# Layer 2's spatial product as seven block products over pairs of row tiles, with its mixer's pools on the other side of the memory

## The chip, the cores and the metric

The kernel runs on one core of a Trainium2 chip. A core has TensorE (PE, with its weight loads PEld), VectorE (DVE), ScalarE (ACT), GpSimd (POOL) and SyncE (SP), which here issues every DMA from one queue in order, and 16 DMA engines. The metric is the device time of one execution in microseconds (us), as the median of repeated runs.

## What is computed

Two layers, each a memory-augmented attention followed by a gated mixer (gMLP), on x of 2048 rows by 640. The change concerns the second layer's mixer:

```
z  = gelu(layernorm(x) @ w_in)        # 2048 x 1728
z1 = z[..., :864]
z2 = layernorm(z[..., 864:])
g  = einsum("ts,bsf->btf", w_sp, z2) + b_sp[None, :, None]     # w_sp 2048 x 2048
x  = x + einsum("bsf,fd->bsd", z1 * g, w_out)                  # w_out 864 x 640
```

Every matrix is split into a high and a low f16 part, and a product is three matmul passes: high by high, high by low, low by high.

## The kernel before

A layer runs in three phases. `phase1a` is the attention. `phase1b` (L234) projects the last four row tiles' attention (`yp`), normalizes each of the 16 row tiles of 128 rows, transposes it by DMA (`th`, L218) and multiplies it with w_in in two halves (`w_in_half`, L294): `z2_half` applies gelu and the layer norm and keeps z2 in SBUF as `zh` and `zl`, `z1_half` stores z1 to memory. TensorE's order is the written one, with the scheduler's moves by priority; the other engines' order is the scheduler's.

`phase2` (L326) goes over the 16 row tiles of w_sp. `rows` loads 128 rows (`wr`, 1 MB, L354), takes each row's largest value (L356) and a power-of-two scale from it (L346 to L361), splits the scaled rows into `wn` in two halves of 1024 columns (ACT L366, DVE L367) and transposes both by DMA into `wt` (L368). `spatial` multiplies: 16 blocks of 128 rows of z2, three passes, two halves of 432 columns, 96 matmuls into `gp` (L379). ACT adds the bias and scale (L382), DVE multiplies with z1 (L384), takes the row's largest value (L386), and ACT and DVE split the result into `un` (L392, L393), which a DMA transposes into `ut` (L395). `tail` multiplies `ut` with w_out (42 matmuls, L408), one tile behind, adds x1 (L411) and stores the output (L412). The next tile's `rows` are issued behind this tile's `spatial`. w_out's parts (`wuh`, `wul`, L106) load at the phase's start.

The pools of `attn_weights` and `kept_tiles` (the attention's weights and state) stay open to the program's end, and layer 2's phases take the memory above them.

## Time and profile before

| | |
|---|---|
| median of 3 runs | 2429.87 us (2422.15 to 2431.55) |
| the profiled execution, its own time | 2432.53 us |
| its span | 2430.8 us, granted clock 0.972 |
| layer 2: last score product of the attention | 1821.28 us |
| layer 2: first matmul with w_in | 1828.69 us |
| layer 2: first matmul of the spatial product | 2035.56 us |
| layer 2: last matmul | 2426.30 us |

The times of the last four rows are starts on TensorE's timeline, from the span's start. In the rows that follow, a name such as `wt<-wn` is the tile written and the tile read; L379 is line 379 of the kernel before. A bracket in a timeline's row gives the idle time of that engine just before it and what ended it. In rows of grouped instructions the count comes first, then busy us, the mean duration in ns, and the idle time before.

### The profile page before, as it was taken

How to read it: one execution, taken by the hardware profiler on the slowest of the kernel's cores; microseconds unless marked ns; L12 is line 12 of the kernel's file. 1: busy time of each engine (PE TensorE's matmuls, PEld its weight loads, DVE VectorE, ACT ScalarE, POOL GpSimd, SP SyncE). 2: the span in 40 equal slices, each digit the busy share in tenths (PEclk: the TensorE clock that was granted, in tenths of full speed). 3: DMA queues.
4: the chain of work that ended last, by engine and by line, in shares of the span. 5: the costliest groups of instructions: out<-in, count | busy, mean ns of one | idle time of the engine just before them, and what ended most of it. 6: DMA issues, size and time to landing. Idle time of an engine off the chain costs nothing. (4 is left out here: it accounts for less than half of the span.)

```text
span 2430.8 us, 50694 instructions
## 1 busy us (share of the span) xinstructions
PE 2222.3 (91%) x20682; PEld 1322.2 (54%) x20682; DVE 1437.1 (59%) x2765; ACT 1133.3 (47%) x1388; POOL 934.0 (38%) x723
## 2 busy tenths in 40 slices
PE   5778899999899999999997989999979997999998
PEld 2445555666555445555654556566654554555554
DVE  7678878776654545444226787887764453444431
ACT  3378688777632322211124987877762221211110
POOL 2178688888610100000002988898871010000000
PEclk9989899999999999999999999999999999999999
DMA  5653545455644388766334354454445345775662
GB/s 158 165 137 98 131 115 132 130 132 135 177 112 128 108 224 200 176 148 163 87 85 106 84 142 121 114 116 110 138 141 127 91 111 153 167 176 152 173 130 54
DMA packets 502505, 325.00 MB, mean 134 GB/s; under 512 B 408512, under 2 KB 443456, under 8 KB 497152
## 3 DMA queue, kind: packets, MB, share of 16 engines
q1 hardware_dynamic: 502272, 321.76, 51.8%
q8 instruction: 162, 2.65, 0.5%
q14 instruction: 71, 0.58, 0.1%
HBM read 148.25 MB, written 85.34 MB: 96 GB/s over the span
## 5 line engine op out<-in xcount | busy, mean ns | idle before, releaser
L975 POOL TENSOR_TENSOR PL<-P,PH 128x1280 f16<-128x1280 f32 x248 | 649.5, 2621 | 112.6 <-ACT PH L974 102.3
L379 PE MATMUL gp<-zh,wt 128*128 128x432 f16 x2048 | 465.3, 347 | 24.3 <-DMA wt<-wn 24.3
L964 DVE TENSOR_REDUCE mx<-mp 128x2 f32<-128x1024 f32 (+3 forms) x512 | 409.2, 817 | 109.7 <-PE mp L920 107.9
L379 PEld LDWEIGHTS <-wt 128*128 128x128 f16 x3072 | 301.1, 98 | 285.5 <-DMA wt<-wn 26.4
L957 ACT ACTIVATE P<-es,sc 128x1024 f32<-128x1024 f32 (+1 forms) x384 | 370.7, 965 | 136.1 <-PE es L920 134.0
L974 ACT CAST PH<-P 128x1280 f16<-128x1280 f32 x256 | 320.6, 1254 | 21.9 <-PE pv L1001 14.7
L294 PEld LDWEIGHTS <-th 128*128 128x128 f16 x1920 | 188.7, 98 | 177.6 <-issue 11.4
L394 POOL MEMSET un<- 128x64 f16 x32 | 4.9, 152 | 706.3 <-DMA ut<-un 645.9
L379 PE MATMUL gp<-zl,wt 128*128 128x432 f16 x1024 | 271.8, 347 | 0.0
L204 POOL TENSOR_TENSOR lnrs<-lnve,mhalf 128x1 f32<-128x1 f32 x92 | 56.5, 622 | 472.7 <-DVE lnve L203 447.6
L948 PEld LDWEIGHTS <-qk 60*128 60x128 f16 (+1 forms) x2048 | 91.3, 94 | 225.0 <-issue 156.2
L356 DVE TENSOR_REDUCE am<-wr 128x1 f32<-128x2048 f32 x32 | 73.2, 2286 | 228.3 <-DMA wr<-in_B_w_sp_dram 228.3
L382 ACT ACTIVATE u<-gp,bsp,un 128x864 f32<-128x864 f32 x32 | 34.2, 1070 | 365.6 <-PE gp L379 365.6
L408 PE MATMUL cyp<-wuh,ut 128*128 128x320 f16 (+1 forms) x896 | 168.4, 305 | 17.4 <-DMA ut<-un 17.4
L948 PE MATMUL mp<-qk 60*128 60x512 f16 (+3 forms) x1024 | 138.8, 308 | 40.7 <-DVE mx L964 39.7
L408 PEld LDWEIGHTS <-ut 128*128 128x128 f16 (+1 forms) x1344 | 133.5, 100 | 77.3 <-DMA ut<-un 19.8
L1001 PE MATMUL pv<-vs,PL 128*128 128x41 f16 x2560 | 164.6, 182 | 8.2 <-DVE PL L975 4.3
L1001 PE MATMUL pv<-vs,PH 128*128 128x41 f16 x2560 | 168.5, 183 | 3.3 <-DVE ab L1017 3.2
L725 PE MATMUL vps<-wvh,xt 128*128 128x320 f16 x640 | 157.5, 313 | 13.1 <-DMA xt<-xnhl 11.9
L920 PEld LDWEIGHTS <-big 64*128 64x128 f16 x3072 | 141.4, 95 | 51.4 <-issue 5.1
L948 PE MATMUL es<-qk 64*128 64x512 f16 (+3 forms) x1024 | 135.3, 300 | 35.3 <-ACT P L957 25.7
L366 ACT ACTIVATE wn<-wr,ivw 128x1024 f16<-128x1024 f32 x64 | 72.0, 1146 | 184.7 <-DVE ivw L361 111.1
(203 smaller groups left out, 4153.6 us busy)
## 6 DMA issues: line engine op xcount, KB each, us to landing
wr<-in_B_w_sp_dram SPq DMA_DIRECT2D x32, 1024.0 KB
...
```

What stands on the lines that cost most here:

```text
L294: nc.tensor.matmul(zp[:, n, :FHH], a[:, k, :], b[:, k, c:c + FHH], start=(k == 0 and j == 0), stop=(k == KD - 1 and j == 2))
L356: nc.vector.tensor_reduce(am, wr, AX.X, ALU.max, apply_absolute_value=True)
L379: nc.tensor.matmul(gp[:, n, :FHH], wt[:, k // 8, a, k % 8, :], b[:, k, n * FHH:(n + 1) * FHH], start=(k == 0 and j == 0), stop=(k == NT - ...
L408: nc.tensor.matmul(yp[:, n, :320], a[:kn[k], k, :], b[:kn[k], k, n * 320:(n + 1) * 320], start=(k == 0 and j == 0), stop=(k == KO - 1 and ...
L725: nc.tensor.matmul(ps, a[:, k, c], b[:, k, n * 320:(n + 1) * 320], start=(i == 0), stop=(i == 14))
L920: nc.tensor.matmul(out, g.big[r, 64 - 64 * s:192 - 64 * s], mk, start=False, stop=s == 1, skip_group_check=True)
L948: nc.tensor.matmul(out[:, h, o:o + w], a[r, ac], b[r, bc], start=o == 0, stop=False, skip_group_check=True)
L957: self.last_of["ACT"] = nc.scalar.activation(P[:, :, 512 * c:512 * c + ew], es[:, :, :ew], AF.Exp, scale=g.esc).ins
L964: self.last_of["DVE"] = nc.vector.tensor_reduce(self.mx[m][:, :, i], mp[:, :, o:o + w], AX.X, ALU.max).ins
L974: nc.scalar.copy(PH, P[:, h])
L975: (nc.gpsimd if h == 0 or n < self.N - self.TAIL else nc.vector).tensor_tensor(PL, P[:, h], PH, ALU.subtract)
L1001: nc.tensor.matmul(pv[:, i, h, :], x[:, c:c + 128], v[:, j, h0 + h, :], start=(j == 0 and x is PH), stop=(j == i and x is PL), skip_group_ ...
```

## The change

Rows and columns of w_sp are paired by tiles: of a pair of row tiles, `a11` and `a12` are the first tile's blocks of even and odd column tiles, `a21` and `a22` the second's. z2 is blocked the same way: even and odd row tiles, and its left and right 432 columns. The 2x2 block product, of eight block products, is done with seven (`product`, 24 matmuls of 432 columns each) on sums and differences of the blocks. The results are joined in PSUM, where some products accumulate on others, and by ACT and DVE (`scaled`, `plus`). For w_sp the four additions of a pair are GpSimd's (`mix`), on rows that ACT has scaled in place, and each of seven blocks is split and transposed by itself (`turned`): seven DMA transposes of a pair, where there were four. For z2 they are made in phase 1b as each tile is finished (`blocks`): seven arrays `zb` in the place of `zh` and `zl`, with four GpSimd differences a pair. Blocks are made seven products ahead of their use; there are eight `wt` buffers, two of `wn`, two of `wr`, one of `un`. SP's order in the new phase is the written one.

Layer 2's attention weights and state are closed when its attention ends (`ats.close()`); phase 1b's pools lie on the other side of the memory, and one tile `w0` over the closed pools holds first half of w_in and later w_out. The first layer is as before.

```diff
+    def place(self, t):
+        n = self.nk * self.cols
+        self.h, self.l = [t[:, i, :n].rearrange("p (k c) -> p k c", k=self.nk) for i in range(2)]
...
-def phase1b(g, o_d, x, x1_d, z1_d, zh, zl):
+def phase1b(g, o_d, x, x1_d, z1_d, put, w0=None):
     nc, tc = g.nc, g.tc
+    zs = ZS if w0 is None else ZB
     with ExitStack() as ctx:
         pool = lambda n, b, **k: ctx.enter_context(tc.tile_pool(name=n, bufs=b, reuse_waits="tile", **k))
-        p2, p1, px2, px1, sp = pool("b2", 2), pool("b1", 1), pool("bx2", 2), pool("bx1", 3 if g.wi[0].made else 1), pool("bs", 2)
-
-        pe2, pe1, wp0 = pool("be2", 2), pool("be1", 1), pool("bw0", 1)
+        if w0 is None:
+            p2, p1, px2, px1, sp = pool("b2", 2), pool("b1", 1), pool("bx2", 2), pool("bx1", 1), pool("bs", 2)
+            pe2, pe1, wp0 = pool("be2", 2), pool("be1", 1), pool("bw0", 1)
+        else:
+            right = lambda n, b: pool(n, b, side="right")
+            pe2, pe1, p2, p1, px2, px1, sp = right("be2", 2), right("be1", 1), right("b2", 2), right("b1", 2), right("bx2", 2), right("bx1", 3), None
...
         ctx.enter_context(tc.manual_schedule(engines=ENGINES))
-        g.wi[0].tiles(wp0)
-        with tc.high_priority(offset=HP):
+        if w0 is None:
+            g.wi[0].tiles(wp0)
+        else:
+            g.wi[0].place(w0)
+        with tc.high_priority(offset=HP if w0 is None else 2 * HP):
...
             z2 = p1.tile([128, FH], F32, tag="z2", name="z2")
-            nc.scalar.activation(z2.rearrange("p (n c) -> p n c", n=2), zp[:, :, :FHH], AF.Gelu_apprx_tanh, scale=g.zi[1])
-            layernorm(g, z2, z2, FH, 2, ZS)
-            nc.scalar.copy(zh[:, t, :], z2)
-            nc.vector.tensor_tensor(zl[:, t, :], z2, zh[:, t, :], ALU.subtract)
+            i = nc.scalar.activation(z2.rearrange("p (n c) -> p n c", n=2), zp[:, :, :FHH], AF.Gelu_apprx_tanh, scale=g.zi[1])
+            j = layernorm(g, z2, z2, FH, 2, zs)
+            put(t, z2, p1)
+            return i.ins, j.ins
...
-            z2_half(t, w_in_half(1, *th))
+            last = z2_half(t, w_in_half(1, *th))
+            if i == 11:
+                g.mark = last
...
+def blocks(g, zb):
+    nc = g.nc
+    even = {}
+    def put(t, z, pool):
+        j = t // 2
+        l, r = z[:, :FHH], z[:, FHH:]
+        def keep(b, src):
+            nc.scalar.copy(zb[b][:, 0, j], src)
+            nc.vector.tensor_tensor(zb[b][:, 1, j], src, zb[b][:, 0, j], ALU.subtract)
+        def diff(nm, a, b):
+            o = pool.tile([128, FHH], F32, tag=nm, name=nm)
+            nc.gpsimd.tensor_tensor(o, a, b, ALU.subtract)
+            return o
+        if t % 2 == 0:
+            keep(0, l)
+            t1 = diff("zt1", r, l)
+            keep(3, t1)
+            even[j] = r, t1
+            return
+        r0, t1 = even.pop(j)
+        keep(1, l)
+        keep(2, r)
+        t2 = diff("zt2", r, t1)
+        keep(4, t2)
+        keep(5, diff("zt3", r, r0))
+        keep(6, diff("zt3", l, t2))
+    return put
...
+def phase2s(g, w_sp, x1_d, z1_d, zb, w0, out):
+    nc, tc = g.nc, g.tc
+    KO, NP = 7, NT // 2
+    RING = 8
+    kn = [128] * 6 + [FH - 768]
+    ks = [0, 1, 2, 3, 6, 7, 4, 5]
+    with ExitStack() as ctx:
+        pool = lambda n, b, **k: ctx.enter_context(tc.tile_pool(name=n, bufs=b, reuse_waits="tile", **k))
+        pr, ph, ps = pool("dr", 2), pool("dh", 2), pool("ds", 2)
+        p1, p2, pv = pool("d1", 1), pool("d2", 2), pool("dv", 1)
+        pt = pool("dtr", 1, side="right")
+        pg, py = pool("dg", 1, space=PSUM), pool("dy", 1, space=PSUM)
+        ctx.enter_context(tc.manual_schedule(engines=ENGINES | {mybir.EngineType.SP}))
...
+        def rows(p):
+            w = []
+            for t in (2 * p, 2 * p + 1):
+                wr = pr.tile([128, S], F32, tag="wr", name="wr")
+                nc.sync.dma_start(wr, w_sp[t * 128:(t + 1) * 128, :])
+                am = small("am")
+                nc.vector.tensor_reduce(am, wr, AX.X, ALU.max, apply_absolute_value=True)
...
+                nc.scalar.activation(wr, wr, AF.Identity, scale=iv)
+                v = wr.rearrange("p (m i c) -> p i m c", i=2, c=128)
+                w.append((v[:, 0], v[:, 1]))
+            def turned(src):
+                hl = ph.tile([128, 2, 1024], F16, tag="wn", name="wn")
+                v = hl.rearrange("p l (m c) -> p l m c", c=128)
+                nc.scalar.copy(v[:, 0], src)
+                nc.vector.tensor_tensor(v[:, 1], src, v[:, 0], ALU.subtract)
+                wt = pt.tile([128, 2, NP, 128], F16, tag=f"wt{cnt[0] % RING}", name="wt")
+                cnt[0] += 1
+                nc.sync.dma_start(wt.rearrange("p l k c -> p (l k) c"), hl.rearrange("p l c -> p (l c)"), transpose=True)
+                return wt
+            def mix(a, b, op, o=None):
+                if o is None:
+                    o = ps.tile([128, 1024], F32, tag="s", name="s").rearrange("p (m c) -> p m c", c=128)
+                nc.gpsimd.tensor_tensor(o, a, b, op)
+                return o
+            (a11, a12), (a21, a22) = w
+            yield turned(a11)
+            s1 = mix(a21, a22, ALU.add)
+            yield turned(s1)
+            s2 = mix(s1, a11, ALU.subtract)
+            yield turned(s2)
+            yield turned(a12)
+            yield turned(mix(a11, a21, ALU.subtract, a21))
+            yield turned(a22)
+            yield turned(mix(a12, s2, ALU.subtract, a12))
+        def product(o, wt, b, start=True):
+            for i, m in enumerate(ks):
+                for j, (x, y) in enumerate(((0, 0), (0, 1), (1, 0))):
+                    nc.tensor.matmul(o[:, :FHH], wt[:, x, m, :], zb[b][:, y, m, :], start=start and i == j == 0,
+                                     stop=i == NP - 1 and j == 2, skip_group_check=True)
...
+        def scaled(o, a, un, t):
+            nc.scalar.activation(o, a[:, :FHH], AF.Identity, bias=g.bsp[:, t:t + 1], scale=un)
+        def plus(o, a, un, b):
+            nc.vector.scalar_tensor_tensor(o, a[:, :FHH], un, b, ALU.mult, ALU.add)
...
+            hl = p1.tile([128, 2, 128 * KO], F16, tag="un", name="un")
+            ut = p2.tile([128, 2, KO, 128], F16, tag="ut", name="ut")
...
+        todo = (o for p in range(NP) for o in rows(p))
+        with tc.high_priority(offset=HP), ExitStack() as held:
+            for i in g.mark:
+                held.enter_context(tc.issue_after(i))
+            wt = [next(todo) for _ in range(7)]
...
+        woh, wol = g.wu.place(w0)
+        for _ in g.wu.load(None):
+            pass
+        pend = []
+        for p in range(NP):
+            t = 2 * p
+            bank = lambda nm: pg.tile([128, 512], F32, tag=nm, name="g" + nm)
+            vec = lambda nm: pv.tile([128, FHH], F32, tag=nm, name=nm)
+            u, u1 = [p2.tile([128, FH], F32, tag="u", name="u") for _ in range(2)]
+            pa, pb, pc, pd = [bank(nm) for nm in "abcd"]
+            v, v1, q, q1 = [vec(nm) for nm in ("v", "v1", "q", "q1")]
+            def step(o, b, start=True):
+                product(o, wt.pop(0), b, start)
+                wt.extend(islice(todo, 1))
...
+            un, un1 = scales[p]
+            step(pa, 0)
+            scaled(v, pa, un, t)
+            scaled(v1, pa, un1, t + 1)
+            step(pc, 3)
+            if pend:
+                tail(*pend.pop(0))
+            step(pb, 4)
+            plus(q, pb, un, v)
+            if pend and p + 1 < NP:
+                tail(*pend.pop(0))
+            z1 = [fetch("z1", i, z1_d[i]) for i in (t + 1, t)]
+            step(pa, 1, False)
+            scaled(u[:, :FHH], pa, un, t)
+            step(pb, 5, False)
+            plus(q1, pb, un1, v1)
+            plus(u1[:, FHH:], pc, un1, q1)
+            x1 = [fetch("x1", i, x1_d[i]) for i in (t + 1, t)[:1 + (p + 1 < NP)]] + [None]
+            step(pd, 6)
+            plus(u1[:, :FHH], pd, un1, q1)
+            pend.append((*gate(t + 1, u1, z1[0]), x1[0]))
+            step(pc, 2, False)
+            plus(u[:, FHH:], pc, un, q)
+            pend.append((*gate(t, u, z1[1]), x1[1]))
+        for x in pend:
+            tail(*x)
...
+    ats = ExitStack()
+    attn_weights(g, ats, wv, wq, wk, wo, w_in, w_out)
...
+    kept = kept_tiles(g, ats)
...
+                if i:
+                    ats.close()
+                    w0 = zs.enter_context(tc.tile_pool(name="w0", bufs=1, reuse_waits="tile")).tile([128, 2, 7 * D], F16, name="w0")
                 zp = zs.enter_context(tc.tile_pool(name="z2", bufs=1, reuse_waits="tile"))
-                zh = zp.tile([128, NT, FH], F16, name="zh")
-                zl = zp.tile([128, NT, FH], F16, name="zl")
-                phase1b(g, o_d[i], xs[i], x1_d[i], z1_d, zh, zl)
-            phase2(g, w_sp, x1_d[i], z1_d, zh, zl, xs[i + 1], att[1] if i == 0 else None)
+                if i:
+                    zb = [zp.tile([128, 2, NT // 2, FHH], F16, name=f"zb{j}") for j in range(7)]
+                    phase1b(g, o_d[i], xs[i], x1_d[i], z1_d, blocks(g, zb), w0)
+                else:
+                    zh = zp.tile([128, NT, FH], F16, name="zh")
+                    zl = zp.tile([128, NT, FH], F16, name="zl")
+                    phase1b(g, o_d[i], xs[i], x1_d[i], z1_d, whole(g, zh, zl))
+            if i:
+                phase2s(g, w_sp, x1_d[i], z1_d, zb, w0, xs[i + 1])
```

Three places in the order of instructions. First TensorE at the end of layer 2's attention (`pv` is a score product with the values, `zp` the product with w_in). Before:

```order
L1001 LDWEIGHTS PH_26616
L1001 MATMUL pv_26627<-vs_16370,PH_26616 128x41
L1001 LDWEIGHTS PL_26617
L1001 MATMUL pv_26627<-vs_16370,PL_26617 128x41
L294 LDWEIGHTS th_26754
L294 MATMUL zp1_26770<-wi1h_19436,th_26754 128x432
```

Now, with the last head pair's products `pv_26627` behind and between those of the first half tile:

```order
L308 LDWEIGHTS th_26759
L308 MATMUL zp1_26775<-wi1h_19436,th_26759 128x432
L1222 LDWEIGHTS PH_26592
L1222 MATMUL pv_26627<-vs_16370,PH_26592 128x41
L308 LDWEIGHTS th_26759
L308 MATMUL zp1_26775<-wi1h_19436,th_26759 128x432
```

25 matmuls of the half tile stand ahead of the first of these rows' `pv` and five more before its second matmul, where all 30 stood behind the last. The loads of this tile's and the next tile's x1 rows, their layer norms and transposes moved with it, into the attention.

Second SP in the middle of the second phase. Before, one tile:

```order
L374 DMA cz_29593<-z_1_6 128x864
L395 DMA_TRANSPOSE ut<-un 128x14x128
L412 DMA out_dram<-xo 128x640
L403 DMA cx_29734<-x_1_5 128x640
L354 DMA wr<-in_B_w_sp_dram 128x2048
L368 DMA_TRANSPOSE wt<-wn 128x16x128 x2
```

Now, from the end of one pair into the next:

```order
L482 DMA_TRANSPOSE ut<-un 128x14x128
L435 DMA_TRANSPOSE wt<-wn 128x16x128
L482 DMA_TRANSPOSE ut<-un 128x14x128
L417 DMA wr<-in_B_w_sp_dram 128x2048 x2
L435 DMA_TRANSPOSE wt<-wn 128x16x128 x2
L498 DMA out_dram<-xo 128x640
L435 DMA_TRANSPOSE wt<-wn 128x16x128
L498 DMA out_dram<-xo 128x640
L469 DMA cz_29600<-z_1_5 128x864
L469 DMA cz_29602<-z_1_4 128x864
L435 DMA_TRANSPOSE wt<-wn 128x16x128 x2
```

The two row loads stand behind both gate transposes of the pair before, and the seven block transposes stand between the other transfers one or two at a time.

Third DVE in the same place, the gate of a tile. Before:

```order
L384 TENSOR_TENSOR u<-u,cz_29971 128x864
L359 TENSOR_SCALAR un<-pw 128x1
L386 TENSOR_REDUCE uam<-u 128x1
L346 TENSOR_SCALAR pw<-uam 128x1
L347 TENSOR_SCALAR pw<-pw 128x1
```

Now, the odd tile's gate first, with the even tile's and the sixth block's subtraction (`wn`) between:

```order
L473 TENSOR_TENSOR u<-u,cz_30374 128x864
L475 TENSOR_REDUCE uam<-u 128x1
L407 TENSOR_SCALAR upw<-uam 128x1
L408 TENSOR_SCALAR upw<-upw 128x1
L465 SCALAR_TENSOR_TENSOR u<-gc,un,q 128x432
L409 RECIPROCAL uiv<-upw 128x1
L484 TENSOR_SCALAR xs<-upw,pw 128x1
L473 TENSOR_TENSOR u<-u,cz_30376 128x864
L410 TENSOR_SCALAR uiv<-uiv 128x1
L432 TENSOR_TENSOR wn<-wr,wn 128x1024
L475 TENSOR_REDUCE uam<-u 128x1
L480 SCALAR_TENSOR_TENSOR un<-u,uiv,un 128x864
```

The odd tile's last step (`un`) stands behind three operations for the even tile and the sixth block.

55 lines of the change are left out of this document (52 added, 3 removed).

## The prediction

> **What bounds the kernel now.** I read the page first, then the busy time of each stretch of layer 2's mixer, then what TensorE waited for, and the timelines last. The page's first part, and its largest TensorE group:
>
> ```profile
> PE 2222.3 (91%) x20682; PEld 1322.2 (54%) x20682; DVE 1437.1 (59%) x2765; ACT 1133.3 (47%) x1388; POOL 934.0 (38%) x723
> L379 PE MATMUL gp<-zh,wt 128*128 128x432 f16 x2048 | 465.3, 347 | 24.3 <-DMA wt<-wn 24.3
> ```
>
> TensorE is busy for 91% and its largest group is the spatial product that the change rewrites in layer 2. The stretches of layer 2's second phase (the stretch, then its length, busy time and count of PE, PEld, DVE, ACT and POOL, the granted clock, the DMA share, GB/s):
>
> ```profile
> 2022.00:2036.00 14.00, 1.11 (x6) 0.40 (x5) 3.53 (x3) 3.22 (x4) 0.00 (x0) 0.71 0.93 276
> 2036.00:2155.00 119.00, 111.45 (x631) 62.06 (x630) 54.50 (x97) 23.95 (x23) 0.76 (x5) 0.98 0.74 176
> 2155.00:2405.00 250.00, 250.00 (x1483) 144.88 (x1482) 93.17 (x158) 39.79 (x38) 1.67 (x11) 1.00 0.56 138
> 2405.00:2431.00 26.00, 16.85 (x97) 10.39 (x95) 5.56 (x10) 2.09 (x2) 0.00 (x0) 0.86 0.16 43
> ```
>
> From 2155 to 2405 TensorE has no gap and every other engine is under 40%: there a matmul left out is worth its issue time, for as long as whoever feeds TensorE keeps up. At the edges it waits. TensorE's waits, the first three from 1808 to 1836 (the attention's end), the last two from 2022 on (us in total, times, longest):
>
> ```profile
> PE zp L294 <- DMA th<-xnhl: 7.2, 1, 7.2
> PE pv L1001 <- DVE PL L975: 4.3, 1, 4.3
> PE pv L1001 <- POOL PL L975: 2.3, 1, 2.3
> PE gp L379 <- DMA wt<-wn: 13.4, 3, 12.9
> PE cyp L408 <- DMA ut<-un: 11.9, 4, 4.9
> ```
>
> The sum below is made against the span of 2430.8 us. That execution took 2432.53, 2.7 above the median of 2429.87 (2422.15 to 2431.55), so I take the difference off the median.
>
> **The matmuls removed.** A whole tile in TensorE's timeline, and a whole output product:
>
> ```profile
> 2319.99 0.53 PE L379 MATMUL gp<-zh,wt 128*128 128x432 f16 x2
> 2337.51 0.43 PE L408 MATMUL cyp<-wuh,ut 128*128 128x320 f16 x2
> ...
> 2077.31 0.45 PE L408 MATMUL cyp<-wuh,ut 128*128 128x320 f16 x2 [2.91 <-DMA ut<-un]
> 2083.03 0.53 PE L379 MATMUL gp<-zl,wt 128*128 128x432 f16 x2
> ```
>
> 96 spatial matmuls take 17.52 us (0.1825 each), the 42 of the output 5.72, so two tiles cost 46.5. The change has 7 products of 24 matmuls for a pair, 168 in place of 192: 30.7 + 11.4 = 42.1. Over eight pairs that is 192 matmuls fewer, **-35.0**.
>
> **The attention's end.** As the order shows, 25 of the 30 matmuls of the first half tile now stand ahead of the last score products and five among them, and that tile's x1 row and layer norm stand far earlier. So the 7.2 falls away, and the 4.3, since that DVE subtraction stood behind a layer norm which waited 5.5 us for x1:
>
> ```profile
> 1818.30 0.89 DVE L201 BATCH_NORM_STATS2 lnst<-x 128x6 f32<-128x320 f32 x2 [5.50 <-DMA x<-x]
> ```
>
> The 2.3 is filled too. These are 13.8, and the half tile's own 5.5 fill what is left: **-15**, with -10 as the low side (the 4.3 stays). Behind it phase 1b is TensorE's. Its seven block casts and subtractions a pair replace two wide ones each on ACT and DVE, busy for 28% and 47% there (54.31 and 90.36 of 192 us in the row quoted next), and the extra GpSimd differences find 173 us free: 0, at worst +6, if the first row blocks' three GpSimd additions hold up one layer norm.
>
> ```profile
> 1830.00:2022.00 192.00, 192.00 (x1075) 105.54 (x1074) 90.36 (x190) 54.31 (x62) 19.02 (x30) 0.99 0.40 101
> ```
>
> **Start of the spatial product.** Today the first transposes stand on SP behind the loads of w_out, and TensorE waits 12.9. The change puts two of seven ahead of the last z1 store, and the third is not needed for 8.8 us: **-13**.
>
> **The feeding loop.** This decides. Each pair now needs seven transposed blocks in place of four, and of the row buffers there are just two, so the next pair's rows load only when the last block of this one is made; on SP they stand behind both gate transposes (ut). I call W the issue of the two row loads and follow the chain round. The prices:
>
> ```profile
> 2175.10 4.96 SPq L368 DMA_TRANSPOSE wt<-wn  x2
> 2179.66 1.15 ACT L366 ACTIVATE wn<-wr,ivw 128x1024 f16<-128x1024 f32 x1 [3.48 <-DMA wt<-wn]
> 2181.89 1.15 ACT L366 ACTIVATE wn<-wr,ivw 128x1024 f16<-128x1024 f32 x1 [0.18 <-DMA wt<-wn]
> 2183.29 1.52 SPq L395 DMA_TRANSPOSE ut<-un  x1
> 2186.54 0.42 SPq L354 DMA_DIRECT2D wr<-in_B_w_sp_dram  x1
> 2187.38 0.15 POOL L394 MEMSET un<- 128x64 f16 x1 [25.50 <-DMA ut<-un]
> 2193.55 2.29 DVE L356 TENSOR_REDUCE am<-wr 128x1 f32<-128x2048 f32 x1 [8.41 <-DMA wr<-in_B_w_sp_dram]
> 2188.80:2191.60 2.80, 2.80 (x18) 1.50 (x16) 0.00 (x0) 0.00 (x0) 0.00 (x0) 1.00 0.94 358
> L303 DVE TENSOR_TENSOR zl<-z,zh 128x864 f16<-128x864 f32 x15 | 15.9, 1059 | 8.7 <-ACT zh L302 8.7
> L302 ACT CAST zh<-z 128x864 f16<-128x864 f32 x16 | 14.6, 914 | 53.2 <-DVE z L210 53.2
> L384 DVE TENSOR_TENSOR u<-u,cz 128x864 f32<-128x864 f32 x15 | 15.8, 1056 | 59.8 <-ACT u L382 59.8
> L386 DVE TENSOR_REDUCE uam<-u 128x1 f32<-128x864 f32 x15 | 15.8, 1053 | 0.1
> L392 ACT ACTIVATE un<-u,uivw 128x864 f16<-128x864 f32 x15 | 15.1, 1005 | 11.4 <-DVE uivw L389 11.4
> L393 DVE SCALAR_TENSOR_TENSOR un<-u,uivw,un 128x864 f16<-128x864 f32 x15 | 16.7, 1113 | 3.7 <-ACT un L392 3.7
> ```
>
> A block lands 4.6 us after its issue (2175.10 to 2179.66), two in a row 6.8, a gate transpose 4.1 (2183.29 to 2187.38), a row load 7.0 (2186.54 to 2193.55), and a second megabyte at 358 GB/s 2.9 later. By elements, a cast of 1024 is 1.08 and its subtraction 1.26. From W = 0: rows there at 7.0 and 9.9; the second maximum ends at 12.2, small operations at 12.9; ACT scales both rows in place, 4 x 1.15 = 4.6, to 17.5; the first block is cast and subtracted, to 19.8, and issued; it lands at 24.4. Blocks have two buffers, so the third is cast only now: issue 26.7, landing 31.3; so the fifth, 33.6. DVE then runs in its order (shown above) the odd tile's product with z1, its maximum, half a microsecond of small ones, an output half (0.6), the even tile's product, the sixth block, the even maximum and the odd `un`: 1.06 + 1.05 + 0.5 + 0.6 + 0.2 + 1.06 + 1.26 + 1.05 + 1.11 = 7.9, to 41.5. The odd gate transpose lands at 45.6. `un` has one buffer, so the even tile's cast and subtraction follow, to 47.7, and with SP's 1.5 for its transpose the next rows are issued at **49.2**. TensorE's turn is 42.1: it waits 7.1 in every round, at the output product of the odd tile, whose ut comes 3.6 ahead of W. DVE, ACT and SP are each idle for a third of it; the time is in the chain. Six rounds, the first with 5.0: **+40.5**.
>
> The first two rounds are worse. The last five blocks of pair 0 follow each other at one landing for two, to 20 us behind phase 1b's last matmul; w_out's loads follow (1.9 MB, 5.4 us), so pair 1's rows are issued at 21.5 and its first block lands at 49.3, while TensorE is through with pair 0 at 31.2: **+18**. The chain from there brings pair 0's first ut to 71.3, against TensorE at 58.1: **+13**.
>
> Gone are today's waits of 11.9 and the rest of 13.4: **-12.4**. A long wait also costs clock. Behind a gap:
>
> ```profile
> 2036.98 1.50 PE L379 MATMUL gp<-zh,wt 128*128 128x432 f16 x4
> 2038.32 0.53 PE L379 MATMUL gp<-zl,wt 128*128 128x432 f16 x2
> ...
> 2418.99 1.27 PE L408 MATMUL cyp<-wuh,ut 128*128 128x320 f16 x4
> 2420.06 0.74 PE L408 MATMUL cyp<-wul,ut 128*128 128x320 f16 x2
> ```
>
> Four matmuls take 1.34 and 1.07 us where they take 0.73 and 0.55, for 2.5 and 6 us: 1.2 and 2.9 lost. Two such gaps go and two come (about 0). In the six rounds the loss eats into the next wait.
>
> By the Trainium skill (TensorE: Matmul & The Clock Gate, Part 1), an idle window of about 3.4 us halves the clock for about as long: 1.7 a wait. The trace agrees within a factor of two. It speaks against the change, whose waits all pass that length; with them hidden the sum stands, and unhidden it would be six times 1.7, 10 us, slower.
>
> **Sum**: -15 - 13 - 35.0 + 40.5 + 18 + 13 - 12.4 = -3.9; 2429.9 - 3.9 = **2426 us**. The loop is the open cost. Low end: every row as its fastest (a lone row load landed in 5.6: 1957.92 to 1963.48) and DVE's run not in the way, 46; high end: two of the landings cost what a second transpose costs (6.8 for 4.6), 53.6. I take 49.2, since the rows are those of the same operations. Six rounds by these ends give 2407 to 2452.
>
> ```profile
> 1957.92 0.34 SPq L354 DMA_DIRECT2D wr<-in_B_w_sp_dram  x1
> 1963.48 2.29 DVE L356 TENSOR_REDUCE am<-wr 128x1 f32<-128x2048 f32 x1 [1.26 <-DMA wr<-in_B_w_sp_dram]
> 2176.30:2178.60 2.30, 2.30 (x19) 1.66 (x18) 2.23 (x5) 0.00 (x0) 0.00 (x0) 1.00 1.11 202
> ```
>
> The last row is a transpose in flight: 202 GB/s, so 2.6 us for its 0.52 MB. The Trainium skill (DMA: Bandwidth & Descriptors, Latency and other measured facts) has 261 GB/s for such a transpose, 2.0 us; the trace is below it. By the page's figure four landings a round would be 0.6 shorter, and the sum about 14 us lower; by the row it stands.
>
> **Rivals.** (1) *The loop nearly closes* at 46 or less, since ACT casts and landings overlap better than my serial count: six rounds gain 19 or more, 2407 and below. For it: no engine is full. Against: the single `un` buffer and the pairs of block buffers are real waits. (2) *Transposes crowd the queues*, and the change is slower. A pair moves 3.7 MB of blocks and 0.9 of gates at 202 GB/s (23 us) and 4.3 MB of rows, z1, x1 and output at 358 (12): 35 of 49 us of DMA, 0.71 against 0.56 now. If each of the four landings on the chain comes 1.2 later, the round is 54 and the first two rounds 5 each longer: 2426 + 29 + 10 = 2465. It decides from a round of about 52. For it: a transpose behind another took 6.8. (3) *The half tile doesn't fill the attention's end*, because some added load holds SP or DVE there: 2441.
>
> **Chances.** Forecast (2418 to 2442, a change that cannot be told from none, as 0.5% is 12 us here) 0.34; rival 1 0.27; rival 2 0.35; rival 3 0.04, inside the same bounds. So faster 0.27, same 0.38, slower 0.35. The range for 8 in 10 takes in the loop's ends and part of either rival: 2400 to 2464; the forecast's own is 2418 to 2442.
>
> **What would show it.** TensorE's waits after phase 1b should be led by the output product on ut, about 5 to 7 us once a pair; one wait of 18 at pair 1's first product, on wt. SP should be found waiting for DVE at blocks 3, 5 and 6 and at ut. The first w_in matmul should start before 1816 and the first spatial one within a microsecond of the last z1 half. If TensorE runs without gaps, or the wait is on blocks and not on ut, the loop is wrong.

## The result, and the profile after

| | before | after | ratio |
|---|---|---|---|
| median (4 runs each) | 2426.57 us | 2454.19 us | 1.0105, 95% from 1.0068 to 1.0143 |
| a second set (7 and 4 runs) | 2424.50 us | 2452.69 us | 1.0112, 1.0093 to 1.0131 |
| profiled execution: time, span, granted clock | 2432.53, 2430.8, 0.972 | 2444.19, 2442.3, 0.967 | |

The change makes the kernel slower by 1.0% to 1.1%. The forecast was no change: 2426 us. The measured time lies inside the range of 2400 to 2464, but 28 us off, and a slower kernel had been given 0.35. Since the kernel before measured 2424 to 2427 here and not 2429.9, the change itself is off by some 30 us: -4 was forecast, +26 to +28 came. The profiled execution of after is its fastest of four: its layer 2 began 5.1 us earlier than in the profile of before, in work that is the same in both. So stretches are compared below, not ends.

The page of after, its first part (busy time and instructions of each engine):

```profile
PE 2198.3 (90%) x20490; PEld 1305.8 (53%) x20490; DVE 1554.6 (64%) x2869; ACT 1197.7 (49%) x1476; POOL 1066.6 (44%) x787
```

The 192 matmuls are gone (20682 before), and TensorE's busy time fell by 24 us. VectorE, ScalarE and GpSimd took on 118, 64 and 133 us. The waits of TensorE in the last part of layer 2's attention and in phase 1b, from 1600 to 2040 (us in total, times, longest): first the rows of before that the prediction did not show, then the longest of after.

```profile
PE mp L948 <- DVE mx L964: 2.8, 3, 1.8
PE es L948 <- DMA qk<-mr: 2.6, 2, 2.1
PE pv L1001 <- DVE ab L1017: 1.2, 1, 1.2
```

```profile
PE ga L458 <- DMA wt<-wn: 4.6, 1, 4.6
PE mp L1169 <- DVE mx L1185: 4.4, 3, 3.1
PE es L1169 <- DMA qk<-mr: 4.0, 2, 2.0
PE zp L308 <- DMA th<-xnhl: 3.5, 2, 2.5
PE zp L308 <- DVE ab L1238: 2.6, 1, 2.6
PE mtp L1203 <- DVE gm L1078: 1.7, 1, 1.7
```

Before's 7.2, 4.3 and 2.3 us are gone, 13.8 as forecast. But the score products (`mp`, `es`) wait 8.4 us for 5.4, `mtp` 1.7, the w_in products (`zp`) 3.5 for `th` in other places, and the wait for `ab` is 2.6 for 1.2: 9.6 of the 13.8 came back. From the first score product with the values in layer 2 to the last w_in matmul the timelines give 693.0 us before, 687.6 after and 691.0 in the second profile of after: 2 to 5 us gained, where 15 were forecast.

Behind phase 1b, the waits of TensorE from 2008 to 2443:

```profile
PE cyp L494 <- DMA ut<-un: 33.5, 6, 13.2
PE ga L458 <- DMA wt<-wn: 19.0, 2, 14.4
PE gc L458 <- DVE u L465: 14.5, 8, 4.3
```

The list is led by the output product on `ut`, as forecast, with one wait of 14.4 us at pair 1's first product (forecast 18). The third row was not forecast. Phase 1b's last matmul to the span's end takes 430.4 us, and 432.7 in the second profile of after (408.5 before; 419.6 by the forecast's terms). This whole stretch, first of before, then of after (length, then busy time and count of PE, PEld, DVE, ACT and POOL, granted clock, DMA share, GB/s), and two parts of it in after:

```profile
2022.50:2430.80 408.30, 378.91 (x2209) 217.57 (x2208) 156.56 (x267) 68.55 (x65) 2.43 (x16) 0.97 0.60 148
```

```profile
2012.10:2442.30 430.20, 356.58 (x2017) 202.40 (x2016) 232.54 (x327) 116.05 (x112) 85.89 (x46) 0.93 0.69 167
```

```profile
2012.00:2088.00 76.00, 43.84 (x220) 22.19 (x219) 36.84 (x49) 23.25 (x25) 16.55 (x9) 0.82 0.78 182
2289.00:2339.00 50.00, 44.42 (x252) 25.35 (x252) 30.00 (x42) 14.96 (x14) 11.53 (x6) 0.94 0.74 178
```

The first 76 us hold 44 of matmuls. From then on each round takes about 50 us, of which TensorE is busy for 44, and no other engine is over 60%: the loop is bound by what its engines wait for from each other, as forecast. One round on SP's timeline of after (start, us in the queue):

```profile
2292.86 1.61 SPq L417 DMA_DIRECT2D wr<-in_B_w_sp_dram  x2
2311.96 5.14 SPq L435 DMA_TRANSPOSE wt<-wn  x2
...
2318.70 1.93 SPq L435 DMA_TRANSPOSE wt<-wn  x1
...
2334.89 1.54 SPq L482 DMA_TRANSPOSE ut<-un  x1
2336.53 2.67 SPq L435 DMA_TRANSPOSE wt<-wn  x1
2341.44 1.30 SPq L482 DMA_TRANSPOSE ut<-un  x1
2342.78 1.80 SPq L417 DMA_DIRECT2D wr<-in_B_w_sp_dram  x2
```

From W = 2292.86: first block at +19.1 (forecast 19.8), third at +25.8 (26.7), odd gate transpose at +42.0 (41.5), even one at +48.6 (47.7), next rows at +49.9 (49.2).

### The profile page after: what moved, and what is told of

Same layout as the page of the kernel before. It is cut to its first block, busy times and chain, and to the rows that moved or that the text cites. A ratio compares the mean times of both kernels' runs of the same rounds, so it can differ in the third digit from the quotient of the medians.

```text
span 2442.3 us, 50615 instructions
## 1 busy us (share of the span) xinstructions
PE 2198.3 (90%) x20490; PEld 1305.8 (53%) x20490; DVE 1554.6 (64%) x2869; ACT 1197.7 (49%) x1476; POOL 1066.6 (44%) x787
## 4 chain that ended last, share of the span: by engine, by line
PE 24%; DMA 8%; DVE 7%; ACT 5%; issue 3%; POOL 2%; SPq 1%; ACTq 0%; DVEq 0%; POOLq 0%
PE zp L308 6%; DMA wt<-wn 2%; PE cyp L494 2%; PE pv L1222 2%; PE yps L979 2%; PE kps L1003 1%; PE gb L458 1%; DMA ut<-un 1%; DVE wn L432 1%; PE mp L1169 1%; PE qps L1003 1%; ACT PH L1195 1%; ACT P L1178 1%; DMA wr<-in_B_w_sp_dram 1%; PE vps L946 1%
## 5 line engine op out<-in xcount | busy, mean ns | idle before, releaser
L600 PE MATMUL gp<-zh,wt 128*128 128x432 f16 x1024 | 235.2, 350 | 10.6 <-DMA wt<-wn 10.6
L600 PEld LDWEIGHTS <-wt 128*128 128x128 f16 x1536 | 151.8, 99 | 143.8 <-DMA wt<-wn 11.4
L458 PEld LDWEIGHTS <-wt 128*128 128x128 f16 x1344 | 133.4, 99 | 153.3 <-issue 25.2
L1169 PE MATMUL mp<-qk 60*128 60x512 f16 (+3 forms) x1024 | 138.4, 307 | 42.6 <-DVE mx L1185 41.5
L308 PE MATMUL zp<-wi1h,th 128*128 128x432 f16 x640 | 149.4, 348 | 4.4 <-DMA th<-xnhl 4.3
L1222 PEld LDWEIGHTS <-PH 128*128 128x128 f16 x2560 | 142.3, 96 | 18.6
L1222 PEld LDWEIGHTS <-PL 128*128 128x128 f16 x2560 | 143.1, 97 | 3.8 <-POOL PL L1196 2.1
L600 PE MATMUL gp<-zl,wt 128*128 128x432 f16 x512 | 137.6, 351 | 0.0
L494 PE MATMUL cyp<-w,ut 128*128 128x320 f16 (+1 forms) x672 | 103.4, 318 | 36.0 <-DMA ut<-un 33.5
```

The source lines that it names most:

```text
L308: nc.tensor.matmul(zp[:, n, :FHH], a[:, k, :], b[:, k, c:c + FHH], start=(k == 0 and j == 0), stop=(k == KD - 1 and j == 2))
L458: nc.tensor.matmul(o[:, :FHH], wt[:, x, m, :], zb[b][:, y, m, :], start=start and i == j == 0, stop=i == NP - 1 and j == 2, skip_group_che ...
L494: nc.tensor.matmul(yp[:, n, :320], a[:kn[k], k, :], b[:kn[k], k, n * 320:(n + 1) * 320], start=(k == 0 and j == 0), stop=(k == KO - 1 and ...
L600: nc.tensor.matmul(gp[:, n, :FHH], wt[:, k // 8, a, k % 8, :], b[:, k, n * FHH:(n + 1) * FHH], start=(k == 0 and j == 0), stop=(k == NT - ...
L1169: nc.tensor.matmul(out[:, h, o:o + w], a[r, ac], b[r, bc], start=o == 0, stop=False, skip_group_check=True)
L1222: nc.tensor.matmul(pv[:, i, h, :], x[:, c:c + 128], v[:, j, h0 + h, :], start=(j == 0 and x is PH), stop=(j == i and x is PL), skip_group_ ...
```

## The experiments

The ratios are to the kernel before on the same chip, in the same set of runs. "Round" is the time from one pair's row loads to the next pair's, as the mean of the four or five in the middle of the phase (after: 50.2 us); "attention and 1b" is the stretch of 687.6 us above.

### Set 1: is the round a chain through the single `un` and the pairs of block buffers?

after_again is the changed kernel as it is.

> The changed kernel as it is, for its spread and a second profile. The first profiled run took 2444.19 us, but the other three 2452 to 2456. Theory A (the closed chain from the row loads to the next row loads sets the round, 49.9 us in the first profile): the round in a second profile is 49.5 to 51 as well, and a run that is 8 to 10 us longer has its rounds longer by 1.3 to 1.7 each, in DMA landings. Rival B (TensorE's clock): the longer run shows the same chain and a lower granted clock.

It measured 1.0112 (1.0093 to 1.0131), with six rounds (first to seventh even gate transpose on SP) in 302.3 us, for 301.4 in the first profile. So the 12 us more of this profile's span are not in the rounds: 6.3 lie ahead of layer 2, 3.4 in its attention and 1b, 2.3 behind. Its granted clock is 0.965 for 0.967, too little to tell cause from effect.

A second buffer for `un`:

```diff
-            hl = p1.tile([128, 2, 128 * KO], F16, tag="un", name="un")
+            hl = p2.tile([128, 2, 128 * KO], F16, tag="un", name="un")
```

> Only the gate's half-precision copy gets a second buffer (3.5 KB more). Theory A: the even tile's gate transpose no longer waits for the odd one's landing, goes out right behind block 7 (2339.2 instead of 2341.4 in the first profile's round), and the round shortens by about 2.2: six rounds, -13 us, about 2440 where the changed kernel measures 2453. Rival B (TensorE's own turn with the cold clock and the waits on VectorE fill the round): within 3 us of the changed kernel. Rival C (the queues are the limit): within 3 us too, with the gate transposes landing later.

1.0101 (1.0084 to 1.0118). Over five rounds the even gate transpose came 1.8 us earlier in the round, the odd one 0.2 later, and the round is 49.2 us: 1 us of it gained.

The next pair's row loads ahead of the last gate transpose on SP (`load` holds the two loads that `rows` had):

```diff
             step(pc, 2, False)
+            if p + 2 < NP:
+                load(p + 2)
             plus(u[:, FHH:], pc, un, q)
```

> Only the order on SP: the next pair's two row loads stand behind block 7 and ahead of the even tile's gate transpose, not behind it. Theory A: rows are issued at 2339.2 instead of 2342.8 in the first profile's round, 3.6 earlier, six rounds, -20 us: about 2433 where the changed kernel measures 2453; the even gate transpose may land up to 3 later behind 2 MB of rows, which TensorE sees only if its output product comes within that (it is 12 us behind the odd one). Rival B: within 3 us. Rival C (queues): gate transposes land 3 to 6 later and the gain is under 8 us.

1.0121 (1.0106 to 1.0136); rounds of 50.7 us. Nothing gained.

A third buffer for the split blocks, with one ring buffer fewer to make room:

```diff
-    RING = 8
+    RING = 7
-        pr, ph, ps = pool("dr", 2), pool("dh", 2), pool("ds", 2)
+        pr, ph, ps = pool("dr", 2), pool("dh", 3), pool("ds", 2)
```

> The block buffers from two to three; the ring of transposed blocks from eight to seven to make room. Theory A: the third and the fifth block no longer wait for the first's and third's landing; the odd gate transpose goes out 3 to 4 earlier in the round and so do the next rows: six rounds of -3 and 3 to 8 us at the first two rounds, -20 to -26 us, 2427 to 2433 where the changed kernel measures 2453. Rival B: within 3 us. Rival C (queues): landings of the blocks grow from 4.5 to 6 us as three are in flight, and the gain is under 8 us.

1.0104 (1.0089 to 1.0119); rounds of 50.2 us. The third block was issued at the same place as before, +26.0. Why, the casts of the third block show, first of after, then of wn3 (ScalarE's timelines), and behind them wn3's VectorE:

```profile
2316.33 1.04 ACT L431 CAST wn<-s 128x1024 f16<-128x1024 f32 x1 [3.83 <-DMA wt<-wn]
```

```profile
2318.28 1.05 ACT L431 CAST wn<-s 128x1024 f16<-128x1024 f32 x1 [2.06 <-POOL s L441]
```

```profile
2316.25 6.38 DVE L432 TENSOR_TENSOR wn<-s,wn 128x1024 f16<-128x1024 f32 x2 [0.21 <-ACT wn L431]
```

In after the cast waits for a buffer; with a third buffer it waits for GpSimd's sum, and VectorE's two subtractions take 6.38 us where one alone takes 1.23. Two chains of about the same length lie beside each other here. So in the rounds a link taken away by itself gains next to nothing: theory A, as I had put it, link by link, falls there. In the first two rounds wn3, with one ring buffer fewer too, does gain what theory A said (3 to 8 us): pair 1's rows are issued 19.4 us behind phase 1b's last matmul and not 25.3, and the first output product starts at 70.4 and not 75.8. Its phase behind 1b takes 425.9 us.

### Set 2: rows a pair ahead, the attention's end, the ring's place

pr4 gives the rows four buffers. A pair's rows load and are scaled one pair ahead, so the long first part of the chain (19 us to the first block) lies beside the pair before. Room comes from a ring of seven and from sums and outputs made in place.

```diff
+        raw, made = {}, {}
+        def load_rows(p): ...
+        def scale_row(t): ...
             step(pa, 0)
+            if p + 2 < NP:
+                load_rows(p + 2)
...
             step(pd, 6)
+            if p + 2 < NP:
+                made[p + 2] = [scale_row(t) for t in (2 * p + 4, 2 * p + 5)]
```

> Four row buffers in place of two, so that a pair's rows are loaded a whole pair ahead of its first block, and their maxima and scales stand before the pair's gates; room is made by one ring slot less (7), by taking the difference s2, the sums q and the output in the place of their operands. Three chains of nearly equal length were seen in the changed kernel's round: (a) rows, maxima, blocks, gate transposes, rows; (b) the odd tile's output product, its VectorE sum, behind which the row maxima stand, scales, blocks, gate transpose, that product again; (c) SP's own queue from block 1 to the odd gate transpose, 23 us of which SP is idle for 2.5. Theory A2 (the row loads and maxima on chains a and b make the round; c alone is 23 us and fits in 42): rounds fall from 50.2 to 42.5 to 44, TensorE's own turn, and the wait of 15 at pair 1's first product mostly goes: -45 to -60 us, 2395 to 2410 where the changed kernel measures 2453. Rival D (SP's queue or the DMA engines limit it: 30 us of issue and some 35 us of transfers a round): rounds stay at 48 or more, gain under 20 us.

1.0036 (1.0020 to 1.0051). Rounds fall to 46.5 us and not to 42.5 to 44. The first blocks come late: the first spatial product starts 14.5 us behind phase 1b's last matmul, 4.9 in after. I put it down to the block buffers' place, over tiles that phase 1b still uses; pr4s_hold4, below, moves them.

hold4 holds VectorE's part of the first two layer norms of layer 2's phase 1b until the attention's fourth pair from the end (`g.amark`, set in the attention, not shown). The second tile's load stays at its place (1679.20; 1672.89 in after):

```diff
-            xn = attn_out(ts[0], *a)
+            h = ExitStack(); w0 is not None and h.enter_context(tc.issue_after(g.amark)); xn = attn_out(ts[0], *a)
             a = load(ts[1])
-            th = xn_t(xn)
+            th = xn_t(xn); h.close()
```

> Only the first two tiles' layer norms of layer 2's mixer are held back until the attention's fourth pair from the end, instead of standing in VectorE's and SP's order some 100 to 170 us earlier; TensorE's order is unchanged. Theory E: in the changed kernel these layer norms wait for their x1 rows in VectorE's queue ahead of the score maxima, which cost TensorE 2.2 us near 1620 and 6.3 near 1685 of the earlier kernel's clock (the score products slip by this against the earlier kernel in both profiles); held back, the slip goes: -6 to -8.5 us, about 2445 where the changed kernel measures 2453. Rival: the slip only moves to the attention's end, where the first half tile then waits for its layer norm: within 3 us.

1.0105 (1.0092 to 1.0118), against 1.0112 for after in set 1: not told apart. In its timeline the slip at the second layer norm (see below) is gone, but the score products lose 4.0 us near 1750, where after loses 2.1, and 1.5 more near 1796, where VectorE now runs the held layer norms. Attention and 1b take 687.4 us: the loss moved. With pr4:

> The four row buffers and the held layer norms together. If both theories hold their gains add, since one lies in the attention and the other behind phase 1b: -51 to -68 us, 2385 to 2402, which would be faster than the kernel before by 1 to 1.6 per cent. If SP's queue or the DMA engines are the limit: above 2425.

0.9999 (0.9989 to 1.0010), below pr4's 1.0036 in the same set, 8 us in the medians. pr4_hold4's profile has 4.7 us less in attention and 1b (683.4 for 688.1), but also 5.0 less behind them, where the edit changes nothing, so how much the edit gained stays open.

perm_4 turns the places of the ring's buffers by four and leaves the order of instructions as it is:

```diff
-        cnt, scales = [0], {}
+        cnt, scales = [0], {}; [pt.tile([128, 2, NP, 128], F16, tag=f"wt{i}", name="wt") for i in [4, 5, 6, 7, 0, 1, 2, 3]]
```

> Only the places of the eight ring slots are turned round by four, so that the first block's slot doesn't lie over the last input tile of phase 1b; no instruction is moved. Theory F: in the changed kernel SP holds block 1 until phase 1b's last matmul (8.4 us of waiting, released by TensorE) because its slot lies over that tile, and so the first spatial product starts 4.9 us late; with the slots turned, block 1 goes out about 9 us earlier, the first product starts within 1 us of phase 1b's end, and pair 1's rows 2 to 4 us earlier: -2 to -4 us over all. Rival: block 1 was held by its cast or by SP's order: nothing changes, within 1 us in the trace.

1.0127 (1.0114 to 1.0140). The first spatial product starts without its wait of 4.6 us, so the place was its cause. On SP's list of after it is this row, the first ring buffer over phase 1b's input tile:

```profile
SPq L435 <- PE zp L308: 8.4, 1, 8.4
```

But pair 1's first block still lands 52.5 us behind phase 1b's last matmul, TensorE waits 15.6 for it instead of 14.4, and the first output product starts at 76.3 (75.8 in after): the wait only moved.

### Set 3: VectorE's order, the lock with GpSimd, the pools' place

un2_early_amfirst joins un2 and early, and holds the last output sum (`xo`) behind the row maxima, which had stood behind it in VectorE's order:

```diff
+            with tc.issue_after(ams[-1]):
                 nc.vector.scalar_tensor_tensor(xo, yp[:, :, :320], xs, ...)
```

> Two row buffers as in the changed kernel, with the second gate buffer and the earlier row loads of the two runs before, and in addition the output's sum on VectorE is held behind the next rows' maxima. In those two runs the round stayed at 49.7 to 51 although rows were issued earlier, and the trace showed the row maxima standing behind the odd tile's output sum, which waits for TensorE's output product. Theory A3 (two chains of nearly equal length, one through the gate buffer and the row loads, one through that output product and VectorE's order): with both opened the round falls to about 46 (19.4 from the rows' issue to block 1's, 22.8 of SP's queue to the odd gate transpose, 2.6 for block 7, 1.3): six rounds, -20 to -25 us, 2428 to 2433 where the changed kernel measures 2453. Rival D (SP's queue or the DMA engines): rounds stay at 49 to 50, gain under 6 us.

1.0156 (1.0138 to 1.0173), rounds of 51.2 us: worse than un2 and early alone. Theory A3, that the round falls to 46 with both chains opened, fell with it.

dvemix makes the block sums on VectorE:

```diff
-                nc.gpsimd.tensor_tensor(o, a, b, op)
+                nc.vector.tensor_tensor(o, a, b, op)
```

> Only the four sums and differences of row blocks move from GpSimd to VectorE. In the changed kernel a VectorE block subtraction of 1024 takes 2.0 to 3.3 us while GpSimd runs one of these (2.36 to 3.3 us), and 1.23 alone; the last tiles of phase 1b show the same, and TensorE waits 1.3 and 2.9 there for a layer norm. Theory G (the two engines slow each other): VectorE's subtractions go back to 1.23, the two waits in phase 1b shrink by 2 to 4 together, and a round changes by -1 to +2, since VectorE takes on four operations of 1.1 to 1.3 us and loses 4 us of slowing: -6 to +5 us over all. Rival: the slow subtractions have another cause and stay slow: +10 us or more, as VectorE gets 4 x 1.1 us more in each round.

1.0124 (1.0106 to 1.0142). VectorE in phase 1b, first of after, then of dvemix:

```profile
1979.34 2.98 DVE L224 TENSOR_TENSOR xnhl<-xn,xnhl 128x640 f16<-128x640 f32 x1
1982.24 3.37 DVE L432 TENSOR_TENSOR wn<-wr,wn 128x1024 f16<-128x1024 f32 x1
```

```profile
1985.30 0.82 DVE L224 TENSOR_TENSOR xnhl<-xn,xnhl 128x640 f16<-128x640 f32 x1
1986.04 1.22 DVE L432 TENSOR_TENSOR wn<-wr,wn 128x1024 f16<-128x1024 f32 x1
```

Without GpSimd beside it the subtraction takes 0.82 in place of 2.98 and the other 1.22 in place of 3.37. TensorE's waits on `th` there fall from 3.5 to 0.4 us, and attention and 1b take 686.2 us. The loop pays it back: rounds of 51.5 us, with the sums on VectorE in line with everything else.

pr4s_hold4 gives pr4_hold4's two added row buffers a pool of their own behind the block buffers, so that the block buffers lie where phase 1b is done earlier, and loads pair 1's rows after block 1:

```diff
-        pr, ph, ps = pool("dr", 4), pool("dh", 2), pool("ds", 1)
+        pr, ph, ps, pq = pool("dr", 2), pool("dh", 2), pool("ds", 1), pool("dq", 2)
...
-            wt = [next(todo) for _ in range(7)]
-            load_rows(1)
+            wt = [next(todo)]
+            load_rows(1)
+            wt += [next(todo) for _ in range(6)]
```

> As pr4_hold4, but the two added row buffers are a pool of their own behind the block buffers, so that pair 0's blocks can again be made in phase 1b's last tiles, and pair 1's rows are loaded ahead of pair 0's second block. In pr4_hold4 the first spatial product waited 14.4 us, and the first three waits behind phase 1b came to 44 us, since the block buffers lay over phase 1b's live tiles. Theory A2: the first product starts 5 us behind phase 1b's end, and pair 1's rows no longer wait: the first waits come to 15 to 25 us instead of 44, -15 to -25 us: 2401 to 2411. Rival D (SP's queue): the same seven blocks and 2 MB of rows have to go through SP and the DMA engines first, the waits only move: above 2420.

0.9943 (0.9928 to 0.9957): 14 us less than pr4_hold4 by the ratios, nearly all of it before the third pair: the later rounds are 46.2 us for 46.5. The first spatial product follows phase 1b's last matmul after 0.2 us. The edit does two things, and no run has the buffers' place without the order of the loads.

pr4u_hold4 adds an order for VectorE and ScalarE: both output products one product later, and the casts of blocks 5 to 7 held behind the sum or gate that TensorE waits for (`feed(i)` makes the next block behind instruction `i`):

```diff
             step(pc, 3)
-            if pend:
-                tail(*pend.pop(0))
             step(pb, 4)
             plus(q, pb, un, v)
-            if pend and p + 1 < NP:
+            if pend:
                 tail(*pend.pop(0))
...
-            plus(u1[:, FHH:], pc, un1, q1)
+            feed(plus(u1[:, FHH:], pc, un1, q1))
...
             pend.append((*gate(t + 1, u1, z1[0]), x1[0]))
+            feed(last[-1])
```

> As pr4s_hold4, and the odd tile's output product stands one spatial product later on TensorE, and the casts of blocks 5, 6 and 7 are held behind the sum or gate that TensorE needs first, on VectorE and ACT. In pr4_hold4 the round was 45.4 to 46.5, with 1.5 to 2.4 us of waiting for the odd gate transpose and 1.5 to 2.8 for the sum on gc, both behind a block's subtraction in VectorE's order. Theory H (VectorE's order is what is left): rounds of 42.5 to 43.5, -15 to -20 us against pr4s_hold4: 2383 to 2395. Rival D (DMA): rounds stay above 45.

0.9881 (0.9863 to 0.9899); rounds of 44.7 us. TensorE's longest wait from 2008 on:

```profile
PE cyp L504 <- DVE cx L507: 12.3, 7, 3.2
```

### Set 4: the attention's end by itself, and the best version

The forecast's gain at the attention's end was still open, since every kernel so far had both halves of the change. bound has the moved pools, the new boundary and the earlier layer norms, with the old mixer in layer 2:

```diff
-                phase2s(g, w_sp, x1_d[i], z1_d, zb, w0, xs[i + 1])
...
+            phase2(g, w_sp, x1_d[i], z1_d, zh, zl, xs[i + 1], None if i else att[1])
```

> The other half of the change alone: layer 2 keeps the mixer of the kernel before (four products a pair of tiles, no blocks in phase 1b), and only the pools are moved, over the attention's closed ones, so that the first half tile can fill the attention's end. The prediction priced this part at -15 us. Theory E (the layer norms moved into the attention hold VectorE ahead of the score maxima and give most of it back; 692.9 us from layer 2's first attention product on values to phase 1b's end before, 687.6 to 697.4 in seven profiles with the change): ratio to the kernel before 0.998 to 1.002, that is -5 to +5 us, and the slip of 5 to 6 us at the same place of the attention. Rival (the boundary gain is real and the change loses all of its 26 us behind phase 1b): -10 to -15 us, 2409 to 2414.

0.9949 (0.9935 to 0.9963): 12 us faster than before. The longest of TensorE's waits of bound from 1600 to 2030:

```profile
PE zp L308 <- DMA th<-xnhl: 9.2, 4, 4.4
PE mp L1169 <- DVE mx L1185: 6.0, 3, 3.1
PE es L1169 <- DMA qk<-mr: 4.6, 3, 2.1
```

and all that is left of them from 2008 to the end, and TensorE's timeline where phase 1b ends:

```profile
PE cyp L629 <- DMA ut<-un: 4.9, 1, 4.9
```

```profile
2027.74 3.81 PE L308 MATMUL zp<-w,th 128*128 128x432 f16 x20
2031.39 0.53 PE L600 MATMUL gp<-zh,wt 128*128 128x432 f16 x2
```

The spatial product follows the last w_in matmul directly, and the phase behind it takes 384.1 us in place of 408.5. Attention and 1b, however, take 10.2 us longer than in the profile of before. So bound's gain lies behind phase 1b, and what the attention's end gains is lost again ahead of it: the score products slip as in after (below), and `th` makes TensorE wait 9.2 us in phase 1b. In after the wait on `th` is 3.5. In bound the old mixer's w_out parts and first row loads stand early in phase 1b (1829 to 1901; in before w_out's stand at 2022.70, the first row load at 1957.92), ahead of `th` transposes on SP's queue; SP first, then TensorE:

```profile
1884.74 0.84 SPq L575 DMA_DIRECT2D wr<-in_B_w_sp_dram  x1
1885.68 2.79 SPq L225 DMA_TRANSPOSE th<-xnhl  x1
```

```profile
1892.98 0.90 PE L308 MATMUL zp<-wi1h,th 128*128 128x432 f16 x2 [4.39 <-DMA th<-xnhl]
```

This `th` lands 7.3 us after its issue, and the one before it, also behind a row load, 9.8 (1867.67 to 1877.47). In before the `th` that TensorE waits for at the attention's end lands 3.5 after it (1825.21 to 1828.69).

> As bound, with the two layer norms held until the attention's fourth pair from the end. Theory E: the slip goes and 5 to 8 us come back against bound: 2414 to 2422 where the kernel before measures 2426. Rival: as bound within 3 us.

0.9928 (0.9911 to 0.9946): 5 us below bound in the medians, with intervals that overlap. The slip at the second layer norm is gone here too, and attention and 1b take 695.9 us for 703.1.

pr4v_hold4 is pr4u_hold4 with two PSUM buffers for the output product:

```diff
-        pg, py = pool("dg", 1, space=PSUM), pool("dy", 1, space=PSUM)
+        pg, py = pool("dg", 1, space=PSUM), pool("dy", 2, space=PSUM)
```

> As pr4u_hold4, with a second buffer for the output product's sums (PSUM has two banks free). In pr4u_hold4 the even tile's output product waits 2.2 to 3.5 us in every round for VectorE's sum of the odd one (12.3 us in all), which stands behind a block's subtraction there. Theory H: these waits go and rounds fall from 44.5 to 42.5: -10 to -14 us, 2382 to 2386. Rival D (the DMA engines, whose share is 0.81 in these rounds): the wait moves to the blocks or the gate transpose, gain under 5 us.

0.9855 (0.9838 to 0.9872): 2392.81 us in the median against 2426.03, and the fastest kernel of this study. By the ratios it is 6 us below pr4u_hold4, about half of what was expected, with intervals that overlap, and the rounds of its profile, 44.0 to 47.1 us, are no shorter. The waits on `cx` are gone, but another came in their place. First all that TensorE waits for in pr4v_hold4 from 2089 to 2360, then VectorE's second row maximum of one round and the sum (`u`) behind it:

```profile
PE gc L468 <- DVE u L475: 9.5, 4, 3.7
```

```profile
2233.82 2.29 DVE L426 TENSOR_REDUCE am<-wr 128x1 f32<-128x2048 f32 x1 [1.19 <-DMA wr<-in_B_w_sp_dram]
...
2239.93 0.67 DVE L475 SCALAR_TENSOR_TENSOR u<-gc,un,v 128x432 f32<-128x432 f32 x1
```

By these rows it is still VectorE's order: the sum that TensorE needs stands behind the maxima of the next rows, which wait for their landing. One round's row loads on SP and what follows them, and a stretch of pr4v_hold4 that holds one steady round:

```profile
2223.13 1.65 SPq L418 DMA_DIRECT2D wr<-in_B_w_sp_dram  x2
2225.65 9.90 SPq L445 DMA_TRANSPOSE wt<-wn  x2
```

```profile
2178.00:2223.00 45.00, 42.84 (x258) 25.09 (x257) 25.73 (x42) 14.55 (x14) 9.97 (x6) 1.00 0.91 196
```

Two transposes behind the two row loads now hold SP for 9.8 us, and the DMA share is 0.9 (0.74 in after). TensorE's turn is 42.1. Whether the DMA engines would be the next limit was not tried.

## Why the prediction was right or wrong

The forecast's -3.9 us are -15 ahead of phase 1b's end and +11.1 behind it (408.5 to 419.6). In the two profiles of after the first stretch changed by -5.4 and -1.9, the second by +21.9 and +24.2. So the miss has two halves: 10 to 13 us at the attention's end and in phase 1b, where the mechanism was wrong, and 11 to 13 behind, where the mechanism was right and the terms too small. That the time still lies inside the range of 2400 to 2464 is luck as far as the first half goes: the range was made of the loop's ends and the two rivals of the loop.

bound agrees only in part. Taking the start and today's waits to the boundary, the forecast had -40.4 for it and -35.0 + 40.5 + 18 + 13 = +36.5 for the seven products. Measured, the boundary alone is worth -12 us (3 to 4 either way), and after against bound, 1.0112 over 0.9949, is +40 (some 6 either way). The second number looks right, but it mixes two things: behind phase 1b after takes 46 us longer than bound (430.4 for 384.1), and ahead of it 12 to 16 less, since bound has waits there that after hasn't.

**The matmuls removed, -35.0.** Right in number: 192 fewer. But TensorE's busy time behind phase 1b fell by 22.3 us only (378.91 to 356.58), see the clock below. No experiment times this term alone.

**The attention's end, -15: the step that failed.** The waits that the prediction named did go. What failed is that the layer norms, which the prediction has "far earlier", with their x1 rows and the w_in loads, were costed at nothing in the attention, where they landed: 2 to 5 us were gained in place of 15. VectorE's timeline in after, and the same score maxima in before:

```profile
1675.96 0.89 DVE L208 BATCH_NORM_STATS2 lnst<-x 128x6 f32<-128x320 f32 x2 [1.75 <-DMA x<-x]
...
1677.87 0.66 DVE L1078 TENSOR_TENSOR gm<-num,den 128x480 f32<-128x480 f32 x1
1678.45 2.38 DVE L217 TENSOR_SCALAR xn<-x,lnmv,lnrs 128x640 f32<-128x640 f32 x1
1680.75 1.21 DVE L1185 TENSOR_REDUCE mx<-mp 128x2 f32<-128x1024 f32 x1
```

```profile
1683.56 0.66 DVE L857 TENSOR_TENSOR gm<-num,den 128x480 f32<-128x480 f32 x1
1684.14 1.22 DVE L964 TENSOR_REDUCE mx<-mp 128x2 f32<-128x1024 f32 x1
```

VectorE waits 1.75 us for the x1 row with the score maxima queued behind, and the normalization stands between `gm` and the next maximum. It takes 2.38 us there, ending 0.35 behind a GpSimd operation that ran from 1677.88 to 1680.48; in bound's phase 1b the same operation takes 0.61. Counted from layer 2's first score product with the values, the same score products come 5.5 us later against before in this profile of after, 6.5 in the other and 7.2 in bound. Another 2.1 us go near 1750, where w_in's loads stand earlier on SP; that these are the cause was not tried. In phase 1b some 3 us more go where VectorE's subtractions meet GpSimd's sums (2.98 and 3.37 us above); the prediction had 0 there, at worst 6, and named this case. The slip is shown to come from the layer norm: hold4 and bound_hold4 are without it. What it costs in the end is not shown: without it attention and 1b take 687.4 us in hold4, no less than in after, and 7 less in bound_hold4 than in bound. The rival that this was ("the half tile doesn't fill the attention's end, because some added load holds SP or DVE there") had been given 0.04.

**The start, -13.** TensorE's wait for its first block fell from 12.9 to 4.6, -8.3. perm_4 shows why: the first ring buffer lay over phase 1b's input tile, and SP waited 8.4 us for its last reader. In bound the wait goes whole. The prediction read the order of the instructions, and not what lay under the buffers. Mending it alone gains nothing, as perm_4 also shows.

**Today's waits, -12.4.** With the start, -25.4 was forecast for the phase behind 1b; in bound it is -24.4.

**The first two rounds, +18 and +13.** Right in place (14.4 and 13.2). The first `ut` landed 75.8 us behind phase 1b's last matmul (forecast 71.3), 4.5 later, and pair 1's first block at 51.7 (49.3). The late start does not explain it, since perm_4 has 76.3 without it. The five blocks behind the second kept SP until 22.5 us behind phase 1b's last matmul where 20 was forecast, and wn3, with a third block buffer, has 70.4. With the rows a pair ahead, pr4s_hold4's place and order take 19 us off pr4_hold4's phase (415.4 us to 396.3 in the profiles), of which 1 is in the later rounds.

**The feeding loop, +40.5.** Right within 2%: rounds of 50.2 us for 49.2, links within 1 us. Over six rounds these 2% are 6 to 7 us, 301 to 302 for 295. TensorE waits about 4 us a pair for `ut`, where 7.1 was forecast, and 1.8 for VectorE's sum `u`, which the prediction did not have. And the chain is not single, as I had it. GpSimd's sums, which I had hidden for nothing, run beside it, and four edits of one link each (un2, early, wn3, dvemix) moved a round by 1.3 us or less. Only pr4, which takes the whole first part out of the round, shortens it, to 46.5, and the later output products with VectorE's new order take it to 44.7.

**The clock, about 0.** Too small. In the 76 us at the start the granted clock is 0.82, and 0.94 in the round shown; behind phase 1b it is 0.93 for 0.97 before. Eight of TensorE's turns are 336.8 us at the pace that the prediction counted (42.1 each), and it was busy for 356.58: 20 more, where before lost 7 (371.9 to 378.91). The six rounds hold 13.6 of it (266.2 us busy from 2088 to 2389, for 252.6), 2.3 a round, while the wait in a round came out 1.3 shorter than forecast. That fits "eats into the next wait" for the most part; whether the remaining 1.0 is the clock's or the chain's was not tried.

**Transposes crowd the queues** (the rival, 54 us a round from 0.71 of DMA) did not happen at a share of 0.74. At 0.9, in pr4v_hold4, transposes behind row loads hold SP longer, but TensorE's wait there is VectorE's.

The account: the attention's end and phase 1b missed by 10 to 13 us, the start of the loop by 4.5 to 5, six rounds by 6 to 7. These make 21 to 25 of the some 30. The rest lies within what executions differ: the profile of before, at 2432.53 us, is itself 6 above the median of before's four runs.
